# A kernel of linear attention and four experts: the order of a two-bank product, of a first quarter's copies and of two low halves

## The chip, the cores and the metric

One core of one Trainium2 chip runs the whole kernel. The metric is the device time of one execution in microseconds (us); less is better. Several executions of one kernel are taken and their median is quoted.

## The reference, cut to what matters

```python
def _attn_ref(q, k, v, omega):           # q, k, v: 4 x 8 x 576 x 64; omega: 128 x 64
    q_p, k_p = phi(q * scale), phi(k * scale)   # exp(x omega^T - |x|^2/2 - max)
    kv = einsum('bhsm,bhsd->bhmd', k_p, v); z = sum(k_p, axis=2)
    return einsum('bhsm,bhmd->bhsd', q_p, kv) / (einsum('bhsm,bhm->bhs', q_p, z)[..., None] + 1e-06)

def _moe_ref(x, domain_probs, w1, w2):   # x: 2304 x 512, w1: 4 x 512 x 1024, w2: 4 x 1024 x 512
    p = domain_probs / (domain_probs.sum(-1, keepdims=True) + 1e-09)
    for e in range(4):
        h = np.maximum(x @ w1[e], 0.0)
        out += p[:, e:e + 1] * (h @ w2[e])
```

The attention's output, 2304 tokens by 512, is the x of the experts. All data are float32.

## The kernel before, in words

**Matrix products.** Each float32 operand of an expert is split in two, a high part (rounded, type fp32r) and a low part (what is left), and a product is made of three matmuls: high by high, high by low, low by high. A split is one ACT copy (the high half) and one subtraction on POOL or DVE (the low half).

**Stages.** The tokens are handled in three blocks. The first 512 tokens (with the attention of the first batch) and the next 768 come first, while the other batches' attention runs beside them. The last block, 1024 tokens, is done by `deep` (L1084), and the change is in `deep` alone. `deep` runs eight times, once for each expert and half of its hidden features; the text calls these passes 1 to 8. Pass 1 begins at about 560.4 us, each later one some 39.9 us after the one before it.

**One pass.** Both of the expert's products are made by a scheme of seven products in place of eight, on quarters of the operands. In the last block the second product is turned: the weights are the stationary operand and the hidden values, 512 tokens wide, the moving one, so that a result tile has output features on partitions and fills one PSUM bank (128 x 512 float32). All eight banks come from one pool (L46); a bank is free again when the last instruction that reads it is done, and the oldest free one is given out first.

The order of the work is written out by hand (L1180 to L1298), and every engine runs its instructions in that order. A `product(g, p, where)` (L1107) is six matmuls into a bank; with `start=False` it adds to what the bank holds. The first ten products of a pass are, in order: (0,1), (0,2), (0,5), (0,6), (1,1), (1,2), (0,7), (1,5), (0,3), (0,4); the text counts them first to tenth. The fourth, seventh and tenth add to bank `u` of the first product, with (0,6), (0,7), (0,4). The helpers between them are:

- `keep` (L1119): an ACT copy of a bank to a `sum` tile. `keep(0,"u","u2")` (L1189) copies bank `u` after the fourth product; the seventh product writes that bank and so waits for this copy.
- `added` (L1123) adds a kept sum to a bank on DVE, `scaled` (L1128) takes the maximum with 0 and multiplies by the experts' shares on DVE. They give the quarters a11, a12, a21 and so on. a21 (L1208) reads bank `u` after the seventh product and goes to a new bank; the tenth product writes bank `u` and so waits for a21's `added`.
- `high` (L1134): ACT copy of a quarter, to the high half of a hidden tile (`hs`) or to `r11`. `low` (L1137): the subtraction on DVE that makes the low half.
- `prepare` (L1103): one or no step of the weights' preparation (`w2_sides`, L683) for this pass: ACT copies and POOL subtractions (`w2h`, `w2l`, `w2s`, `w2f`). The steps differ in pass 1 (L1098): there the step behind `keep(0,"b5","p5")` is `plain(3)`, an ACT copy with its POOL subtraction, and in the others it is sums on POOL.

The second product is `times(to, a, b)` (L1140): for two halves f of the hidden features and two banks i, three matmuls each, twelve in all. `into` (L1150) adds the two banks to SBUF tiles on DVE, bank 0 first. The groups in order: `xl` begun with a11 and b11 (L1235, L1240, one f at a time), `xr` from T1 (L1260), `z` (L1265, reads a12 and b12 in `hs[2]` and `hs[3]`), `xr` from A22 (L1272), `xl` left (L1282), `xl` right (L1289), and a last one from T1 with one bank at a time (L1295). The last three use the two banks of `xl` one after the other with `into` in between (L1283, L1290, L1296); the text calls the passages from left to right and from right to last the two junctions. `z` takes two new banks: the first is that which a22 had, the second that which b22 had, so its first matmul waits for the last reader of b22, `low(b22, ...)` (L1257).

```python
        def times(to, a, b, fs=(0, 1), start=True, at=(0, 1)):
            for f in fs:
                (xa, xc), (wa, wc) = a[f], b[f]
                for i in at:
                    ps, w = to[i], slice(i * P, (i + 1) * P)
                    for k, (y, x) in enumerate(((wa, xa), (wa, xc), (wc, xa))):
```

Of the kernel before, what the change touches and what calls it, by code (L numbers as in the profile page):

```python
# [14 lines left out]
def attention_moe(ctx, tc, kT, qT, kd, qd, kn, qn, vn, omT, probs, w1, w2, out):  # L15
# [15 lines left out]
    E, FP, P, _ = w1.shape  # L31
# [36 lines left out]
    def bank(name):  # L68
        return psum.tile([P, 512], F32, tag="ps", name=name)

    def f32(ap):
        return ap.bitcast(F32)
# [34 lines left out]
    def held(shape, tag, dtype=F32R, name=None):  # L107
        return moe.tile(shape, dtype, tag=tag, name=name or tag, bufs=BUFS[tag])
# [531 lines left out]
    def split(t, a, c, hi, lo):  # L640
        if hi is nc.scalar:
            hi.activation(a, t, AF.Copy)  # L642
        else:
            hi.tensor_copy(a, t)
        lo.tensor_tensor(c, t, f32(a), ALU.subtract)  # L645
# [438 lines left out]
    def deep(v):  # L1084
# [4 lines left out]
        hs = [tuple(held([P, n], x) for x in ("hh", "hl")) for _ in range(FH)]  # L1089
# [9 lines left out]
        T1, A22 = ((sevens_t[0][:, i], sevens_t[0][:, i + 1]) for i in (0, 2))  # L1099
        t1, t2 = (x.rearrange("p t c -> p (t c)")[:, :2 * n].rearrange("p (k x) -> p k x", k=2) for x in (va, vb))  # L1100
        r11 = att.tile([P, 2, n], F32, tag="q", name="r11", bufs=1)

        def prepare():  # L1103
            for _ in range(steps2.pop(0)):
                next(ready2, None)

        def product(g, p, where, start=True):  # L1107
            if start:
                P_[g][where] = bank("g1")
            ps = P_[g][where]  # L1110
            (wa, wc), (xa, xc) = W[v, "w1", g][p], X[p]
            for k in range(2):
                w = slice(k * P, (k + 1) * P)
                for a, x, at in ((wa, xa, 0), (wa, xc, 1), (wc, xa, 2)):
                    nc.tensor.matmul(  # L1115
                        ps, a[:, w], x[:, k], start=(start and k + at == 0), stop=(k == 1 and at == 2), skip_group_check=not start
                    )

        def keep(g, where, name):  # L1119
            P_[g][name] = t = held([P, 512], "sum", F32)  # L1120
            nc.scalar.activation(t, P_[g][where], AF.Copy)  # L1121

        def added(g, where, name, to=None):  # L1123
            t = P_[g][where] if to is None else to
            nc.vector.tensor_tensor(t, P_[g][where], P_[g][name], ALU.add)
            return t

        def scaled(t, j):  # L1128
            nc.vector.scalar_tensor_tensor(t, t, 0.0, shares[j], ALU.max, ALU.mult)
# [4 lines left out]
        def high(t, to):  # L1134
            nc.scalar.activation(to, t, AF.Copy)  # L1135

        def low(t, hi, to):  # L1137
            nc.vector.tensor_tensor(to, t, f32(hi), ALU.subtract)  # L1138

        def times(to, a, b, fs=(0, 1), start=True, at=(0, 1)):  # L1140
            for f in fs:
                (xa, xc), (wa, wc) = a[f], b[f]
                for i in at:
                    ps, w = to[i], slice(i * P, (i + 1) * P)
                    for k, (y, x) in enumerate(((wa, xa), (wa, xc), (wc, xa))):
                        nc.tensor.matmul(  # L1146
                            ps, y[:, w], x, start=(start and f + k == 0), stop=(f + k == 3), skip_group_check=not start
                        )
# [35 lines left out]
        prepare()  # L1184
        product(0, 5, "b5")
        keep(0, "b5", "p5")
        prepare()
        product(0, 6, "u", start=False)
        keep(0, "u", "u2")  # L1189
# [2 lines left out]
            store(0)  # L1192
        product(1, 1, "u")
        keep(1, "u", "p1")
        a11 = added(0, "b2", "p1")
        scaled(a11, 0)
        high(a11, hs[0][0])
        high(a11, r11[:, 0])
        low(a11, *hs[0])
        prepare()  # L1200
        product(1, 2, "b2")
        a12 = added(1, "b2", "p1")
        scaled(a12, 0)
        high(a12, hs[2][0])
        low(a12, *hs[2])
        prepare()
        product(0, 7, "u", start=False)
        a21 = added(0, "u", "p5", bank("t"))  # L1208
        scaled(a21, 1)
        prepare()  # L1210
        product(1, 5, "b5")
# [21 lines left out]

        xl = [bank("g2") for _ in range(2)]
        times(xl, hs[:2], weights(0, L), fs=(0,))  # L1235
        product(1, 7, "u", start=False)
        a22 = added(1, "u", "p5", bank("t"))
        scaled(a22, 1)
        less(t2[:, 1], a22, t1[:, 1])
        times(xl, hs[:2], weights(0, L), fs=(1,))  # L1240
        high(a22, A22[0][:, 1])
        split(t2[:, 1], *hs[1], nc.scalar, nc.gpsimd)
# [3 lines left out]
        b22 = added(1, "b5", "u2")  # L1246
# [6 lines left out]
        less(t2[:, 0], b22, t1[:, 0])  # L1253
        split(t2[:, 0], *hs[0], nc.scalar, nc.gpsimd)
        nc.gpsimd.tensor_tensor(r11[:, 0], t2[:, 0], r11[:, 0], ALU.subtract)
        low(b12, *hs[3])
        low(b22, A22[0][:, 0], A22[1][:, 0])  # L1257

        xr = [bank("g2") for _ in range(2)]
        times(xr, split_of(T1), mixed(1, R))  # L1260
        into(xr, 1, 1)
        into(xl, 0, 0)
# [267 lines left out]
    def emit():  # L1530
        pairs, g1 = begin()
        later = [Halves(b, hp) for b in range(1, B) for hp in range(NP)]
        windows = {
            0: (first_rest(pairs, opening(later[0], both=True)), 20 / 11),
            3: (joint_ticks(later[:-NP]), 76 / 45.4),
            N0: (chain(opening(later[-NP]), later_ticks(later[-NP:])), 54 / (NV * (BIG[1][1] // P + 1) * 0.8)),
        }
        ticks, n, done, per = iter(()), 0, 0.0, 0
        for v in range(len(visits)):
            if v in windows:  # L1540
                for _ in ticks:
                    pass
                ticks, per = windows[v]
                n, done = 0, 0.0
            for share in first_visit(g1) if v == 0 else deep(v) if v in DEEP else fast(v) if v >= N0 else plain(v):
                done += share
                while n < done * per:
                    next(ticks, None)
                    n += 1
        store(0)  # L1550
# [62 lines left out]
```

## Time and profile before

| | |
|---|---|
| median of 3 runs | 887.83 us (887.57 to 887.88) |
| the profiled execution | 887.46 us, of which the span from the first to the last instruction is 885.7 us |
| busy, share of the span | PE 99%, PEld 85%, DVE 65%, POOL 63%, ACT 54% |
| granted TensorE clock | 9 tenths or more of full speed in all 40 slices, mean 0.999 |
| chain that ended last | PE 89%, DVE 6%, ACT 2%, issue 2%, DMA 1% |

PE is the matmul engine, PEld its weight loads, DVE VectorE, ACT ScalarE, POOL GpSimd. In a timeline row stand the start, the time taken, engine, line, operation, the tile written and the tiles read, shape and count; in brackets the idle time of that engine before the row and what ended it. The listed 0.39 us of a matmul holds its way through the array; the next one starts before it ends.

### The profile page before, as it was taken

What the parts mean: (1) busy time and instruction counts of PE and PEld (TensorE: products, weight loads), DVE (VectorE), ACT (ScalarE), POOL (GpSimd) and SP (SyncE); (2) the same over time, 40 slices, a digit from 0 to 9 for tenths busy, and PEclk for the clock granted to TensorE, in tenths of its full rate; (3) what the DMA queues carried; (4) which work ended last, traced back from release to release, by engine and by line L of the source; (5) the groups of instructions that cost most, each with busy time, mean ns of one, the idle gap of its engine ahead of it and who ended that gap; (6) DMA issues with size and microseconds to landing.
All of it is one profiled execution on the core that took longest, in us unless ns stands there. A gap on an engine that the chain in (4) does not pass through costs nothing.

```text
span 885.7 us, 13361 instructions
## 1 busy us (share of the span) xinstructions
PE 873.5 (99%) x4785; PEld 749.6 (85%) x4785; DVE 578.4 (65%) x953; ACT 478.4 (54%) x1076; POOL 561.4 (63%) x526
## 2 busy tenths in 40 slices
PE   9999999999999999999999999999999999999997
PEld 9988888989888898898988989777787777777785
DVE  6766566766678537657585576975766748475755
ACT  6696676776765465554555536444343435343341
POOL 6859474655555445344353447778979787887954
PEclk9999999999999999999999999999999999999999
DMA  7664544534422864545545258715525351525312
GB/s 183 195 216 158 190 134 155 176 90 134 134 73 75 306 215 161 214 140 211 195 156 214 78 196 263 260 36 178 154 88 165 98 163 58 179 69 170 121 45 96
DMA packets 67411, 136.04 MB, mean 154 GB/s; under 512 B 10384, under 2 KB 22896, under 8 KB 67344
## 3 DMA queue, kind: packets, MB, share of 16 engines
q1 hardware_dynamic: 57328, 105.05, 37.0%
q0 software_dynamic: 9360, 29.82, 10.3%
q8 instruction: 38, 0.62, 0.3%
q10 hardware_dynamic: 656, 0.31, 0.1%
q14 instruction: 29, 0.24, 0.1%
HBM read 101.06 MB, written 34.10 MB: 153 GB/s over the span
## 4 chain that ended last, share of the span: by engine, by line
PE 89%; DVE 6%; ACT 2%; issue 2%; DMA 1%; SPq 0%; DVEq 0%
PE g L1146 17%; PE g L967 13%; PE g L1115 12%; PE g L830 8%; PE g L831 8%; PE g L832 8%; PE g L815 3%; PE g L816 3%; PE g L817 3%; PE kv L406 2%; PE k_ps L351 1%; DVE acc L1160 1%; PE q_ps L351 1%; PE qt_ps L417 1%; DVE xbl L645 1%
## 5 line engine op out<-in xcount | busy, mean ns | idle before, releaser
L645 POOL TENSOR_TENSOR w2l<-w2r,w2h 128x512 fp32r<-128x512 f32 x61 | 79.2, 1306 | 76.7 <-ACT w2h L642 66.4
L645 POOL TENSOR_TENSOR w1sl<-w1r,w1sh 128x512 fp32r<-128x512 f32 (+1 forms) x43 | 75.1, 1747 | 59.8 <-ACT w1sh L642 53.4
L830 PE MATMUL g<-w2h,hh 128*128 128x512 f32 x280 | 111.7, 399 | 0.0
L832 PE MATMUL g<-w2h,hl 128*128 128x512 f32 x280 | 109.6, 392 | 0.0
L831 PE MATMUL g<-w2l,hh 128*128 128x512 f32 x280 | 109.6, 391 | 0.0
L1160 DVE TENSOR_TENSOR acc<-g,acc 128x512 f32<-128x512 f32 x104 | 67.6, 684 | 37.1 <-PE g L1146 37.1
L645 POOL TENSOR_TENSOR w1al<-w1r,w1ah 128x512 fp32r<-128x512 f32 (+1 forms) x45 | 49.6, 1118 | 60.1 <-ACT w1ah L642 49.3
L842 DVE SCALAR_TENSOR_TENSOR acc<-g,pr,acc 128x512 f32<-128x512 f32 x70 | 51.0, 735 | 28.0 <-PE g L832 27.9
L832 PEld LDWEIGHTS g<-w2h,hl 128*128 128x128 f32 x280 | 52.5, 188 | 11.5
L1121 ACT ACTIVATE sum<-g 128x512 f32<-128x512 f32 x48 | 28.6, 595 | 61.5 <-PE g L1115 61.5
L830 PEld LDWEIGHTS g<-w2h,hh 128*128 128x128 f32 x280 | 52.6, 188 | 10.1
L831 PEld LDWEIGHTS g<-w2l,hh 128*128 128x128 f32 x280 | 52.7, 188 | 8.9
L645 POOL TENSOR_TENSOR w2s<-w2f,w2s 128x512 fp32r<-128x512 f32 x30 | 38.3, 1302 | 25.7 <-ACT w2s L642 25.7
L981 ACT ACTIVATE hh<-sum 128x384 fp32r<-128x384 f32 x48 | 25.0, 524 | 50.5 <-DVE sum L979 50.1
L645 POOL TENSOR_TENSOR t_hl<-va,t_hl 128x1024 fp32r<-128x1024 f32 x16 | 38.7, 2422 | 20.6 <-ACT t_hl L642 20.6
L985 DVE SCALAR_TENSOR_TENSOR hl<-sum,hh 128x384 fp32r<-128x384 f32 x48 | 27.5, 575 | 36.9 <-ACT hh L981 36.2
L303 DVE RECIPROCAL dn<-dn 128x256 f32<-128x256 f32 (+1 forms) x24 | 46.5, 1943 | 6.7 <-ACT dn L297 6.2
L1138 DVE TENSOR_TENSOR hl<-g,hh 128x512 fp32r<-128x512 f32 x32 | 22.0, 688 | 44.2 <-ACT r L1135 38.9
L1115 PE MATMUL g<-xbh,w1sh 128*128 128x512 f32 x128 | 49.9, 390 | 0.0
L1115 PE MATMUL g<-xbl,w1sh 128*128 128x512 f32 x128 | 49.9, 389 | 0.0
L1115 PE MATMUL g<-xbh,w1sl 128*128 128x512 f32 x128 | 49.8, 389 | 0.0
L645 POOL TENSOR_TENSOR w2l<-w1r,w2h 128x512 fp32r<-128x512 f32 x32 | 44.1, 1391 | 6.5 <-ACT w2h L642 6.4
(254 smaller groups left out, 2697.4 us busy)
## 6 DMA issues: line engine op xcount, KB each, us to landing
w1r<-in_w SPq DMA_DIRECT2D x54, 512.0 KB, 3.6
w2r<-in_w SPq DMA_DIRECT2D x76, 256.0 KB, 3.1
kept<-w1sh SPq DMA_DIRECT2D x16, 512.0 KB, 5.0
kept<-w1sl SPq DMA_DIRECT2D x16, 512.0 KB, 5.6
w1sh<-kept POOLq DMA_DIRECT2D x16, 512.0 KB, 5.0
w1sl<-kept POOLq DMA_DIRECT2D x16, 512.0 KB, 5.7
kept<-w1ah SPq DMA_DIRECT2D x16, 384.0 KB, 4.9
kept<-w1al SPq DMA_DIRECT2D x16, 384.0 KB, 4.9
```

Of the source, the lines that this page charges most:

```text
L303: nc.vector.reciprocal(dn, dn)
L645: lo.tensor_tensor(c, t, f32(a), ALU.subtract)
L830: nc.tensor.matmul(ps, ha[:, ts_], wa, start=(c == 0), stop=False)
L831: nc.tensor.matmul(ps, ha[:, ts_], wc, start=False, stop=False)
L832: nc.tensor.matmul(ps, hc[:, ts_], wa, start=False, stop=(c == FH - 1))
L842: nc.vector.scalar_tensor_tensor(acc[i], ps, sc, acc[i], ALU.mult, ALU.add)
L967: nc.tensor.matmul(ps, a[:, w], x[:, k], start=(start and k + at == 0), stop=(k == 1 and at == 2), skip_group_check=not start)
L985: nc.vector.scalar_tensor_tensor(x, y, 0.0, f32(z), ALU.max, ALU.subtract)
L1115: nc.tensor.matmul(ps, a[:, w], x[:, k], start=(start and k + at == 0), stop=(k == 1 and at == 2), skip_group_check=not start)
L1121: nc.scalar.activation(t, P_[g][where], AF.Copy)
L1146: nc.tensor.matmul(ps, y[:, w], x, start=(start and f + k == 0), stop=(f + k == 3), skip_group_check=not start)
L1160: nc.vector.tensor_tensor(t, ps[i], t, ALU.add)
```

## The change

It does three things, all in `deep`. `times` runs over the banks outside and over the halves f inside, so that a bank gets its six matmuls and then the other bank its six. The five lines of a11 (`added`, `scaled`, two `high`, `low`) stand behind `keep(0,"b5","p5")` rather than behind `keep(1,"u","p1")`, and so ahead of the `prepare` behind the third product, of `keep(0,"u","u2")` and of `keep(1,"u","p1")`. Two low halves exchange places with a neighbour: `low(a12)` comes behind a21's `added`, and `low(b22)` ahead of `low(b12)`.

```diff
         def times(to, a, b, fs=(0, 1), start=True, at=(0, 1)):
-            for f in fs:
-                (xa, xc), (wa, wc) = a[f], b[f]
-                for i in at:
-                    ps, w = to[i], slice(i * P, (i + 1) * P)
+            for i in at:
+                ps, w = to[i], slice(i * P, (i + 1) * P)
+                for f in fs:
+                    (xa, xc), (wa, wc) = a[f], b[f]
                     for k, (y, x) in enumerate(((wa, xa), (wa, xc), (wc, xa))):
...
         product(0, 5, "b5")
         keep(0, "b5", "p5")
+        a11 = added(0, "b2", "p1")
+        scaled(a11, 0)
+        high(a11, hs[0][0])
+        high(a11, r11[:, 0])
+        low(a11, *hs[0])
         prepare()
         product(0, 6, "u", start=False)
         keep(0, "u", "u2")
...
         product(1, 1, "u")
         keep(1, "u", "p1")
-        a11 = added(0, "b2", "p1")
-        scaled(a11, 0)
-        high(a11, hs[0][0])
-        high(a11, r11[:, 0])
-        low(a11, *hs[0])
         prepare()
         product(1, 2, "b2")
         a12 = added(1, "b2", "p1")
         scaled(a12, 0)
         high(a12, hs[2][0])
-        low(a12, *hs[2])
         prepare()
         product(0, 7, "u", start=False)
         a21 = added(0, "u", "p5", bank("t"))
+        low(a12, *hs[2])
         scaled(a21, 1)
...
         nc.gpsimd.tensor_tensor(r11[:, 0], t2[:, 0], r11[:, 0], ALU.subtract)
+        low(b22, A22[0][:, 0], A22[1][:, 0])
         low(b12, *hs[3])
-        low(b22, A22[0][:, 0], A22[1][:, 0])
```

## Rows read from the trace of the kernel before

**Rows 1.** The page, part 1: busy us, share and instructions of each engine

```profile
PE 873.5 (99%) x4785; PEld 749.6 (85%) x4785; DVE 578.4 (65%) x953; ACT 478.4 (54%) x1076; POOL 561.4 (63%) x526
```

**Rows 2.** The waits of PE: who waited for whom, total us, times, longest us

```profile
PE g L1146 <- DVE acc L1160: 2.9, 16, 0.2
PE g L1115 <- DVE t L1125: 2.7, 8, 1.0
```

**Rows 3.** Timeline of PE, pass 6: ninth product's last matmul, tenth's first two

```profile
772.76 0.39 PE L1115 MATMUL g<-xbh,w1sl 128*128 128x512 f32 x1
773.40 0.50 PE L1115 MATMUL g<-xbh,w1ah 128*128 128x512 f32 x1 [0.26 <-DVE t L1125]
773.74 0.40 PE L1115 MATMUL g<-xbl,w1ah 128*128 128x512 f32 x1
```

**Rows 4.** Timeline of the weight loads, pass 6: the tenth product's first load

```profile
773.40 0.19 PEld L1115 LDWEIGHTS g<-xbh,w1ah 128*128 128x128 f32 x1 [0.68 <-DVE t L1125]
```

**Rows 5.** Timeline of DVE, pass 6: a11 scaled, a11 low, a21 added

```profile
764.47 0.70 DVE L1129 SCALAR_TENSOR_TENSOR g<-g,share 128x512 f32<-128x512 f32 x1
...
769.35 0.69 DVE L1138 TENSOR_TENSOR hl<-g,hh 128x512 fp32r<-128x512 f32 x1 [4.18 <-ACT r L1135]
...
772.66 0.69 DVE L1125 TENSOR_TENSOR t<-g,sum 128x512 f32<-128x512 f32 x1
```

**Rows 6.** Timeline of ACT, pass 6: keep p5, keep u2

```profile
765.02 0.60 ACT L1121 ACTIVATE sum<-g 128x512 f32<-128x512 f32 x1 [1.08 <-PE g L1115]
766.38 0.60 ACT L1121 ACTIVATE sum<-g 128x512 f32<-128x512 f32 x1 [0.76 <-PE g L1115]
```

**Rows 7.** Timeline of PE, pass 1: seventh product's first matmul, ninth's last, tenth's first

```profile
568.52 0.39 PE L1115 MATMUL g<-xbh,w1sh 128*128 128x512 f32 x1
...
572.38 0.39 PE L1115 MATMUL g<-xbh,w1sl 128*128 128x512 f32 x1
573.74 0.50 PE L1115 MATMUL g<-xbh,w1ah 128*128 128x512 f32 x1 [0.97 <-DVE t L1125]
```

**Rows 8.** Timeline of DVE, pass 1: a11 scaled

```profile
567.84 0.70 DVE L1129 SCALAR_TENSOR_TENSOR g<-g,share 128x512 f32<-128x512 f32 x1
```

**Rows 9.** Timeline of ACT, pass 1: copy of the preparation, a11's two copies

```profile
565.20 0.63 ACT L642 ACTIVATE w2h<-w1r 128x512 fp32r<-128x512 f32 x1
...
568.57 0.60 ACT L1135 ACTIVATE hh<-g 128x512 fp32r<-128x512 f32 x1 [0.55 <-DVE g L1129]
569.06 0.59 ACT L1135 ACTIVATE r<-g 128x512 f32<-128x512 f32 x1
```

**Rows 10.** Timeline of PE, pass 6: third and fourth matmul of z

```profile
786.27 0.40 PE L1146 MATMUL g<-hh,w2l 128*128 128x512 f32 x1
786.63 0.50 PE L1146 MATMUL g<-hh,w2h 128*128 128x512 f32 x1
```

**Rows 11.** Timeline of DVE, pass 6: low(b12), low(b22)

```profile
785.30 0.68 DVE L1138 TENSOR_TENSOR hl<-g,hh 128x512 fp32r<-128x512 f32 x1
785.90 0.68 DVE L1138 TENSOR_TENSOR t_hl<-g,t_hl 128x512 fp32r<-128x512 f32 x1
```

**Rows 12.** Timeline of PE, pass 6, first junction: left's 9th, 12th; right's first, second

```profile
793.39 0.62 PE L1146 MATMUL g<-hh,w2s 128*128 128x512 f32 x2
...
794.08 0.40 PE L1146 MATMUL g<-hh,w2s 128*128 128x512 f32 x1
794.66 0.47 PE L1146 MATMUL g<-hh,w2s 128*128 128x512 f32 x1 [0.18 <-DVE acc L1160]
794.96 0.39 PE L1146 MATMUL g<-hl,w2s 128*128 128x512 f32 x1
```

**Rows 13.** Timeline of DVE, same junction: into xl, both banks

```profile
793.82 1.38 DVE L1160 TENSOR_TENSOR acc<-g,acc 128x512 f32<-128x512 f32 x2 [1.27 <-PE g L1146]
```

**Rows 14.** Timeline of the weight loads, same junction: right's first load

```profile
794.63 0.19 PEld L1146 LDWEIGHTS g<-hh,w2s 128*128 128x128 f32 x1 [0.58 <-issue]
```

**Rows 15.** Timeline of POOL, pass 6: low half of T1, read by xr from T1

```profile
780.11 2.42 POOL L645 TENSOR_TENSOR t_hl<-va,t_hl 128x1024 fp32r<-128x1024 f32 x1 [1.78 <-ACT t_hl L642]
```

## The prediction

> **What bounds the kernel now.** I read the page's first part, then the waits of PE, then timelines around each of those waits. The first shows PE busy for 99% of the span and no other engine above 85% [rows 1]: time can be won only where PE stands still or starts late. The list of who waits for whom names two waits of PE in the last block: 16 times for the addition of `into` and 8 times for an `added` [rows 2]. These are two and one a pass. The totals there are small, because the listed 0.39 us of a matmul covers most of each hole. The holes have to be read from starts: undisturbed, 17 matmuls lie between the seventh product's first and the ninth product's last, from 568.52 to 572.38 us [rows 7], which is 0.227 us from start to start. Whatever is longer is loss. Three holes stand in every pass.
>
> Hole A, before the tenth product: 0.64 us to its first matmul and 0.34 to the second [rows 3], so 0.98 - 2 x 0.227 = 0.53 us lost, in passes 2 to 8 alike to 0.01. In pass 1 the first step is 1.36 us [rows 7], and with the same 0.11 behind it 1.24 us are lost.
>
> Hole B, inside `z`, before its second bank: 0.36 us [rows 10] and the same 0.11, so 0.24 us, eight times.
>
> Hole C, at the two junctions: 0.58 and 0.30 [rows 12], so 0.88 - 0.45 = 0.43 us, 16 times.
>
> The sum is 7 x 0.53 + 1.24 + 8 x 0.24 + 16 x 0.43 = 3.7 + 1.2 + 1.9 + 6.9 = 13.7 us. No more than this can be won, and the change aims at all three.
>
> **The change part by part.** It adds and removes no instruction; everything is order.
>
> *The product by banks.* Now the left group's first bank ends with its 9th matmul, at 793.39, and the addition starts 0.43 us later, at 793.82, and takes 0.69 a bank [rows 12, 13]; so DVE waits for one bank and not for the whole group. PE reaches the right group about 0.23 us after 794.08, and the bank is not free. With six and six, count from the start of a group: its first bank's last matmul starts at 5 x 0.227 = 1.13, the addition at 1.56, ends at 2.25, and PE's next load came 0.12 after an addition's end (794.51 to 794.63) [rows 13, 14]: 2.37. The load wants to start with the 12th matmul, at 2.50. Margin 0.13 us; the second bank has the same. DVE is free, as it idles 1.27 us before that addition [rows 13] and is asked for it 0.68 us sooner. So hole C goes: -6.9 us, with 0 and -6.9 as ends. I take the whole, since each duration is from a row of the very place.
>
> With this order `z` and the `xr` groups meet their second half f after three matmuls and not after six. T1's low half for `xr` ends at 782.53 [rows 15], and `xr` begins 14 matmuls before 786.27 [rows 10], at 783.09. Both halves f come in one instruction, so the order costs nothing; were that cover of 0.5 us gone, PE would wait for the excess in every pass.
>
> *The exchanged low halves.* `z`'s second bank waits for `low(b22)`, which ends at 786.58 [rows 11]. In first place it ends 0.60 sooner, and the bank is wanted three matmuls later: hole B goes. In return `low(b12)` ends at 786.58, and `z` wants it at its fifth matmul, whose load would start with the fourth, at 786.27 + 0.23 = 786.50. It starts at 786.63, as the fourth does now; the sixth matmul then starts at 786.97 in place of 786.95. Cost 0.02 us a pass; the ends are 0 and the 0.24 of today. -1.9 + 0.2 = -1.7 us.
>
> *The first quarter sooner, passes 2 to 8.* Today ACT makes a11's copies behind `keep(1,"u","p1")`; DVE stands 4.18 us before `low(a11)` until 769.35 [rows 5], and a12's and a21's steps queue behind it, so that a21 is added only at 772.66 to 773.35 while the tenth product wants it by 772.76 [rows 3, 5]. After: a11 is scaled by 765.17 [rows 5], ACT starts the copies 0.49 after the row at 765.02 [rows 6] and 0.49 apart [rows 9], done at about 766.6; `low(a11)` is done at 767.3. The first thing DVE then waits for is the sixth product. Its last matmul is 18 before the ninth product's last, so it starts at 772.76 - 18 x 0.227 = 768.68, and a12's `added` follows some 0.43 later (as in [rows 12, 13]), at 769.1, where today DVE is at `low(a11)` until 770.04. `scaled` takes it to 770.6. a21's `added`, now ahead of `low(a12)`, no longer waits for a12's copy on ACT: it runs from about 770.5 to 771.2, some 1.5 us before it is wanted. Hole A goes: -7 x 0.53 = -3.7 us. `keep(0,"u","u2")`, behind the two copies, ends at about 767.1 in place of 766.98 [rows 6]; the seventh product wants it at 768.7. That wait is hidden by the fifth and sixth product. `low(a12)` is wanted by `z` alone, 14 us later.
>
> *The first quarter sooner, pass 1.* Here the cover is missing. a11 is scaled only at 568.54 [rows 8], because DVE still works on the block before; the edit doesn't change that. So ACT, in order, stands before the first copy until 568.57, as today [rows 9]; but now `plain(3)`'s copy and `keep(0,"u","u2")` stand behind it, which today are done before it. The copies start at 568.57 and 569.06 [rows 9], `plain(3)`'s copy at 569.55 (0.63 long, as in [rows 9]), the keep at 570.07, done at 570.67. The seventh product wants to start at 568.52 [rows 7]. It starts at 570.72, and 0.11 more go with the uncovered load: 2.3 us lost, in place of 1.24. The ends: 1.8 if the preparation's copy slips behind the keep, 2.8 if it waits for a buffer as long as it takes. The tenth product is then in time, as 12 matmuls, 2.7 us, lie between the seventh's end and its start. POOL and SP are passed over only here: `plain(3)`'s subtraction and the weights' sums and load behind it come some 4 us later, and their first reader, the `xr` group from T1, only some 10 us after that; I cost them at nothing. In the other passes the step behind a11 has no ACT copy.
>
> A rule to weigh against this: the weight load. In the trace the held matmul's own load starts with the wait's end, at 773.40, and no sooner [rows 3, 4], so each hole has 0.08 to 0.11 us of load on top of the wait, and these are in my sums. The Trainium skill, "TensorE: Matmul & The Clock Gate", section "Architectural detail: the array is 16× 32×32, not 1× 128×128", says that PE's queue pulls weight loads ahead of matmuls in flight; by that a wait would cost itself alone, the holes would give back about 32 x 0.1 = 3.2 us less, an estimate, and the result would be near 879.6. The row speaks against that here, and I keep the row's figure.
>
> **Sum.** -6.9 - 1.7 - 3.7 + (2.3 - 1.24) = -11.2 us. The profiled execution took 887.46 us, which gives 876.3. It is 0.4 under the median of the runs, 887.83, which gives 876.6. I take 876.5.
>
> **The rivals.** *Pass 1 gets no new hole.* If ACT isn't held there, or the preparation's copy and the keep go ahead, the whole 13.7 come: 874.1 to 874.3. Against it speaks that ACT waited for DVE at just this instruction [rows 9].
>
> *The junctions' margin is not there.* 0.13 us is thin. If loads or wake-ups are later by that much, each of the 32 passages from bank to bank (two junctions, two banks, eight passes) uncovers its load, 0.11 us: 3.5 us back, 880.0. All 6.9 back would be 883.4.
>
> *Slower: what I expect of pass 1 happens in every pass.* The mechanism is one queue: the copy of bank `u` behind a11's copies on ACT. It decides against the change where a11 is scaled later than some 1.6 us after today's 765.17. Then eight holes of 2.3 us, 18.4, stand against 13.6 won: 892.3. Against it: only in pass 1 is DVE still busy with another block; from pass 2 on it idles before `low(a11)`.
>
> *Nothing happens:* the engines follow another order than the one written, and the time stays at 887.8. Nothing in the rows speaks for it.
>
> **How the numbers follow.** The forecast, 875.5 to 877.7 with its unknowns (pass 1 between 1.8 and 2.8, hole B between 0 and half), gets 0.70; no hole in pass 1 0.11; the junctions' margin gone in part or whole 0.12; slower 0.03; nothing 0.02; the remaining 0.02 is for several small waits at once. The range takes in the first rival and most of the second: 874.0 to 880.1. About 0.2%, 1.8 us, is what a measurement of this kernel can tell from no change; all cases but the last ones lie far below that: faster 0.95, same 0.02, slower 0.03.
>
> **What the profile should show.** PE's list of waits without `into` in it; the starts at both junctions and inside `z` 0.23 to 0.25 us apart; passes 2 to 8 some 38.3 us from one to the next in place of 39.9; the tenth product unhindered. In pass 1 a wait of PE for the ACT copy of L1121, about 2.2 us long, before the seventh product, and ACT's order there: two copies of a11, one `w2h`, the keep. I am wrong if the junctions still show steps of over 0.3 us, if the keep in passes 2 to 8 ends after the sixth product, or if the granted clock, 0.999 before, is lower in the last block.

## The result and the profile after

The changed kernel took 876.44 us (median of 4 runs, 875.65 to 877.37) against 887.70 us for the kernel before beside it: ratio 0.9877, 95% interval 0.986 to 0.9894. The medians differ by 11.3 us, and by the ratio the change is 1.2% faster. Predicted were 876.5 us, in a range from 874.0 to 880.1. The profiled execution took 876.04 us, its span 874.0.

First the waits of PE in the changed kernel (who waited for whom, total us, times, longest us):

```profile
PE g L1115 <- ACT sum L1121: 2.0, 1, 2.0
PE warm L1312 <- DVE om_r L1303: 1.1, 1, 1.1
PE k_ps L158 <- POOL k L151: 0.9, 1, 0.9
PE g L815 <- DVE hl L822: 0.2, 1, 0.2
```

Both waits of [rows 2] are gone. One new one stands there, for the ACT copy of L1121, once, 2.0 us long; the other three lie ahead of the last block. The chain that ended last shows the same (start, us, what; a stretch that holds the whole of pass 7):

```profile
793.52 14.96 PE g L1115 x66
808.48 1.36 PE g L1146 x6
809.84 1.36 PE g L1115 x6
811.20 1.36 PE g L1146 x6
812.56 2.72 PE g L1115 x12
815.28 16.56 PE g L1146 x72
```

There is no DVE, no ACT and no "issue" left in it: in a later pass PE alone sets the time. To compare kernels without what happens ahead of the last block, which varies by up to 1.3 us between the profiled executions (the block's first matmul starts between 560.37 and 561.62), I use the starts of matmuls: from the first of L1115 to the last of L1146, and from one pass's first to the next's. Before, that is 560.37 to 880.31, 319.94 us; after, 561.04 to 869.79, 308.75: 11.19 less. Passes 2 to 7 (six steps) take 39.93 us each before and 38.33 after, and pass 1 takes 40.62 before and 40.63 after.

**The tenth product, pass 6.** PE's timeline after, to be held against [rows 3]:

```profile
767.02 0.39 PE L1115 MATMUL g<-xbh,w1sl 128*128 128x512 f32 x1
767.25 0.39 PE L1115 MATMUL g<-xbh,w1ah 128*128 128x512 f32 x1
767.48 0.39 PE L1115 MATMUL g<-xbl,w1ah 128*128 128x512 f32 x1
```

The steps are 0.23 and 0.23 where they were 0.64 and 0.34. Pass 6 starts 5.74 us earlier in this trace (755.01, before 760.75); that is the shift to keep in mind in the next two. DVE after, against [rows 5]:

```profile
758.73 0.70 DVE L1129 SCALAR_TENSOR_TENSOR g<-g,share 128x512 f32<-128x512 f32 x1
760.90 0.69 DVE L1138 TENSOR_TENSOR hl<-g,hh 128x512 fp32r<-128x512 f32 x1 [1.47 <-ACT r L1135]
763.44 0.70 DVE L1125 TENSOR_TENSOR g<-g,sum 128x512 f32<-128x512 f32 x1 [1.85 <-PE g L1115]
764.17 0.70 DVE L1129 SCALAR_TENSOR_TENSOR g<-g,share 128x512 f32<-128x512 f32 x1
764.78 0.69 DVE L1125 TENSOR_TENSOR t<-g,sum 128x512 f32<-128x512 f32 x1
765.53 0.69 DVE L1138 TENSOR_TENSOR hl<-g,hh 128x512 fp32r<-128x512 f32 x1
```

The scaling of a11 stands at the same place in the pass as before (758.73 + 5.74 = 764.47). Its low half comes 2.7 us sooner, DVE then waits for PE and no more for ACT, and a21 is added until 765.47, 1.55 us before 767.02. The prediction said some 1.5.

**Pass 1.** PE, ACT and DVE after, against [rows 7 to 9]; the pass begins 0.67 us later in this trace:

```profile
568.98 0.39 PE L1115 MATMUL g<-xbh,w1al 128*128 128x512 f32 x1
571.40 0.50 PE L1115 MATMUL g<-xbh,w1sh 128*128 128x512 f32 x1 [2.03 <-ACT sum L1121]
571.74 0.40 PE L1115 MATMUL g<-xbl,w1sh 128*128 128x512 f32 x1
```

```profile
565.38 0.60 ACT L1121 ACTIVATE sum<-g 128x512 f32<-128x512 f32 x1 [1.60 <-PE g L1115]
569.26 0.60 ACT L1135 ACTIVATE hh<-g 128x512 fp32r<-128x512 f32 x1 [3.28 <-DVE g L1129]
569.75 0.59 ACT L1135 ACTIVATE r<-g 128x512 f32<-128x512 f32 x1
570.23 0.63 ACT L642 ACTIVATE w2h<-w1r 128x512 fp32r<-128x512 f32 x1
570.75 1.09 ACT L1121 ACTIVATE sum<-g 128x512 f32<-128x512 f32 x2
```

```profile
568.52 0.70 DVE L1129 SCALAR_TENSOR_TENSOR g<-g,share 128x512 f32<-128x512 f32 x1
```

This is one wait told by three engines. ACT stands 3.28 us before a11's first copy because DVE scales a11 only until 569.22; the preparation's copy and the copy of bank `u` come behind it, the latter done at 571.35; at 571.40 the seventh product starts, 2.42 us after the matmul before it, and the next follows 0.34 later. Lost: 2.42 + 0.34 - 2 x 0.227 = 2.3 us.

**Inside `z` and at a junction, pass 6**, against [rows 10, 12, 13]. First `z`'s fourth to sixth matmul, then DVE at the two junctions:

```profile
780.21 0.39 PE L1146 MATMUL g<-hh,w2h 128*128 128x512 f32 x1
780.44 0.42 PE L1146 MATMUL g<-hl,w2h 128*128 128x512 f32 x1
780.69 0.39 PE L1146 MATMUL g<-hh,w2l 128*128 128x512 f32 x1
```

```profile
783.81 2.47 DVE L1160 TENSOR_TENSOR acc<-g,acc 128x512 f32<-128x512 f32 x4
786.63 0.69 DVE L1160 TENSOR_TENSOR acc<-g,acc 128x512 f32<-128x512 f32 x1 [0.36 <-PE g L1146]
788.03 0.69 DVE L1160 TENSOR_TENSOR acc<-g,acc 128x512 f32<-128x512 f32 x1 [0.70 <-PE g L1146]
789.42 0.69 DVE L1160 TENSOR_TENSOR acc<-g,acc 128x512 f32<-128x512 f32 x1 [0.70 <-PE g L1146]
```

In `z` the longest step left is 0.25, behind the fifth matmul, which reads `low(b12)`: 0.02 us lost, as worked out. At the junctions the additions now come singly, one every 1.39 us, and DVE idles 0.70 between them: it is PE that sets the beat. The cover worth watching is the 0.36 us before the first of them; the four additions ahead of it end that close. PE has some to spare too: the addition of the left group's first bank ends at 787.32, and the load of the right group's first matmul can start with the left's last, at 787.60.

### The profile page after: what moved, and what is told of

Same layout as the page of the kernel before. It is cut to its first block, busy times and chain, and to the rows that moved or that the text cites. A ratio compares the mean times of both kernels' runs of the same rounds, so it can differ in the third digit from the quotient of the medians.

```text
span 874.0 us, 13367 instructions
## 1 busy us (share of the span) xinstructions
PE 865.7 (99%) x4785; PEld 750.7 (86%) x4785; DVE 577.4 (66%) x953; ACT 478.8 (55%) x1076; POOL 561.1 (64%) x526
## 4 chain that ended last, share of the span: by engine, by line
PE 95%; DVE 2%; DMA 1%; issue 1%; ACT 0%; POOL 0%; SPq 0%; POOLq 0%; DVEq 0%
PE g L1146 18%; PE g L1115 17%; PE g L967 13%; PE g L830 8%; PE g L831 8%; PE g L832 8%; PE g L815 3%; PE g L816 3%; PE g L817 3%; PE kv L406 2%; PE k_ps L351 2%; PE q_ps L351 1%; PE qt_ps L417 1%; DVE xbl L645 1%; PE q_ps L158 1%; PE nd L290 1%
## 5 line engine op out<-in xcount | busy, mean ns | idle before, releaser
L832 PEld LDWEIGHTS g<-w2h,hl 128*128 128x128 f32 x280 | 52.6, 188 | 11.5 <-DVE hl L822 0.2
L1121 ACT ACTIVATE sum<-g 128x512 f32<-128x512 f32 x48 | 28.7, 600 | 47.4 <-PE g L1115 46.7
L1115 PE MATMUL g<-xbh,w1sh 128*128 128x512 f32 x128 | 49.9, 390 | 2.0 <-ACT sum L1121 2.0
L1115 PE MATMUL g<-xbl,w1sh 128*128 128x512 f32 x128 | 49.8, 389 | 0.0
L1115 PE MATMUL g<-xbh,w1sl 128*128 128x512 f32 x128 | 49.8, 389 | 0.0
L979 DVE TENSOR_TENSOR sum<-g,sum 128x384 f32<-128x384 f32 x48 | 26.5, 555 | 32.7 <-PE g L967 27.6
```

The costliest lines, as they stand in the source:

```text
L832: nc.tensor.matmul(ps, hc[:, ts_], wa, start=False, stop=(c == FH - 1))
L1115: nc.tensor.matmul(ps, a[:, w], x[:, k], start=(start and k + at == 0), stop=(k == 1 and at == 2), skip_group_check=not start)
```

## The experiments

All times are medians. "Last block" is the length from the trace of the profiled execution, reckoned as above; 319.94 us before, 308.75 for the changed kernel.

| kernel | us | ratio to before, 95% interval | last block, us | less than before |
|---|---|---|---|---|
| banks alone | 878.32 | 0.9895 (0.9881 to 0.9908) | 311.25 | 8.7 |
| `low(b22)` alone | 885.36 | 0.9975 (0.9966 to 0.9984) | 318.09 | 1.9 |
| `low(a12)` alone | 882.54 | 0.9942 (0.9929 to 0.9954) | 314.97 | 5.0 |
| a11 alone | 884.45 | 0.9967 (0.9955 to 0.998) | 317.17 | 2.8 |
| the change again | 877.03 | 0.9879 (0.9866 to 0.9893) | 310.44 | 9.5 |
| the change without a11 | 873.97 | 0.9846 (0.9833 to 0.986) | 306.95 | 13.0 |
| banks and `low(a12)` | 874.52 | 0.9851 (0.9837 to 0.9864) | 306.68 | 13.3 |
| a11 behind the keep | 874.29 | 0.985 (0.9837 to 0.9864) | 307.03 | 12.9 |
| a11 two steps late | 878.78 | 0.9909 (0.9892 to 0.9926) | 311.81 | 8.1 |
| a11 five steps late | 893.94 | 1.0079 (1.0064 to 1.0094) | 326.38 | -6.4 |

**The product by banks alone.** The two loops of `times` are exchanged, and nothing else of the change is made.

> The product by banks alone. Theory (three separate holes): the holes at the junctions go (16 x 0.43 = 6.9 us), and the one inside z goes too (1.9 us), since the second bank is now wanted three matmuls later and its old release is in time; hole A stays: 887.7 - 8.8 = 878.9 us, with starts of 0.23 us at both junctions and 0.64 before the tenth product. Rival (the hole in z needs the exchange of low halves): 887.7 - 6.9 = 880.8 us, with 0.3 us or more inside z.

Measured: 878.32, the last block 8.7 us shorter. PE's waits name no `into` any more, and hole A is left as it was:

```profile
PE g L1115 <- DVE t L1125: 2.8, 8, 1.0
```

`z` runs without a hole in it; here are its fourth to sixth matmul (PE's timeline):

```profile
782.34 0.39 PE L1146 MATMUL g<-hh,w2h 128*128 128x512 f32 x1
782.57 0.39 PE L1146 MATMUL g<-hl,w2h 128*128 128x512 f32 x1
782.79 0.39 PE L1146 MATMUL g<-hh,w2l 128*128 128x512 f32 x1
```

So the order by banks closes holes B and C both, and the theory stands against its rival.

**The exchange of `low(b22)` and `low(b12)` alone.**

```diff
+        low(b22, A22[0][:, 0], A22[1][:, 0])
         low(b12, *hs[3])
-        low(b22, A22[0][:, 0], A22[1][:, 0])
```

> The exchange of low(b22) and low(b12) alone. Theory: z's second bank is free 0.60 us sooner, the hole in z goes, nothing else: 887.7 - 1.9 = 885.8 us, junctions still 0.58 us. Rival (the hole only moves to the matmul that reads low(b12)): 887.7 us, with a step of 0.3 us at z's later matmuls.

Measured: 885.36, the last block 1.85 us shorter. The hole in `z` is gone (third, fourth and fifth matmul start at 786.05, 786.28 and 786.51), the junctions are as before. The rival, that the hole only moves on, falls.

**`low(a12)` behind a21's `added`, alone.** a11 stays where it was.

```diff
         high(a12, hs[2][0])
-        low(a12, *hs[2])
         prepare()
         product(0, 7, "u", start=False)
         a21 = added(0, "u", "p5", bank("t"))
+        low(a12, *hs[2])
```

> low(a12) behind a21's added, alone; a11 stays in its old place. Theory: a21's added no longer waits for a12's copy on ACT and starts as soon as a12 is scaled, ending near 572.0 in pass-6 terms where it is wanted 0.7 us later; hole A goes in passes 2 to 8 (3.7 us) and in pass 1 as well (1.2 us), with no new hole there: 887.7 - 4.9 = 882.8 us. Rival (hole A comes from a11's late low half and goes only with a11's move): 887.7 us, with 0.6 us still before the tenth product.

Measured: 882.54, the last block 4.97 us shorter. In this kernel's DVE timeline, pass 6, a11's low half is as late as ever, and still a21 is in time, since the next step of DVE no longer waits for ACT:

```profile
767.30 0.69 DVE L1138 TENSOR_TENSOR hl<-g,hh 128x512 fp32r<-128x512 f32 x1 [4.18 <-ACT r L1135]
767.91 0.69 DVE L1125 TENSOR_TENSOR g<-g,sum 128x512 f32<-128x512 f32 x1
768.63 0.70 DVE L1129 SCALAR_TENSOR_TENSOR g<-g,share 128x512 f32<-128x512 f32 x1
769.24 0.69 DVE L1125 TENSOR_TENSOR t<-g,sum 128x512 f32<-128x512 f32 x1
```

a21 is added by 769.93, and the ninth product's last matmul starts at 770.71. One moved line closes hole A in all eight passes. Pass 1 still takes 0.26 us more than the later ones (39.63 against 39.37): a step of 0.33 us stands in it before the product (1,7), which comes back in three kernels below.

**The move of a11's five lines alone.** `low(a12)` stays ahead of a21's `added`.

> The move of a11's five lines alone; low(a12) stays ahead of a21's added. Theory: passes 2 to 8 lose hole A (3.7 us), a21 being added some 0.1 to 0.2 us before it is wanted; pass 1 gets a hole of 2.3 us before the seventh product in place of its 1.24 before the tenth: 887.7 - 3.7 + 1.1 = 885.1 us. Rival (both moves are needed): hole A stays in part, 886.5 to 888.8 us.

Measured: 884.45, the last block 2.77 us shorter (predicted 2.6). Hole A goes in this way too, with less to spare (a21 is added from 771.08 to 771.77 in pass 6, with the ninth product's last matmul at 771.97). PE waits once for the ACT copy, 2.0 us, and pass 1 takes 41.71 us, 1.09 more than before. So each of the two moves closes hole A by itself, and a11's has the price of a new hole.

**The changed kernel again**, beside the next three.

> The changed kernel once more, as the measure for the kernels beside it: 876.4 us by both theories, one hole of 2.3 us before the seventh product of pass 1.

Measured: 877.03 (875.91 to 878.05). Its profiled execution, 878.05, is the longest of them; the last section shows what stands in its pass 1.

**The whole change without a11's move.**

Relative to the changed kernel:

```diff
         keep(0, "b5", "p5")
-        a11 = added(0, "b2", "p1")
-        scaled(a11, 0)
-        high(a11, hs[0][0])
-        high(a11, r11[:, 0])
-        low(a11, *hs[0])
         prepare()
...
         keep(1, "u", "p1")
+        a11 = added(0, "b2", "p1")
+        scaled(a11, 0)
+        high(a11, hs[0][0])
+        high(a11, r11[:, 0])
+        low(a11, *hs[0])
         prepare()
```

> The whole change without the move of a11's lines. Theory: low(a12)'s move alone closes hole A in every pass and ACT is not held in pass 1, so all 13.7 us come: 874.0 us, 2.4 under the changed kernel, with no hole of PE over 0.3 us in the last block. Rival (a11's move is what closes hole A in passes 2 to 8): 876.4 + 3.7 - 2.3 = 877.8 us or more, with 0.6 us before the tenth product.

Measured: 873.97 (873.85 to 874.43), 3.1 us under the changed kernel beside it, and none of its runs reaches into that one's. ACT in pass 1 copies bank `u` at 566.63, ahead of a11, and no wait of PE in the last block is left in the list. The last block is 12.99 us shorter, and the holes held 13.7. The rest is in sight: pass 1 takes 38.84 us and the later ones 38.33, because two small holes open in pass 1, one before the product (1,7) and one in the `xl` group right. They show in the weight loads:

```profile
577.35 0.19 PEld L1115 LDWEIGHTS g<-xbh,w1sh 128*128 128x128 f32 x1 [0.36 <-ACT sum L1121]
594.42 0.19 PEld L1146 LDWEIGHTS g<-hl,w2s 128*128 128x128 f32 x1 [0.50 <-POOL hl L645]
```

Their matmuls start 0.32 and 0.46 us after the ones before them, so the expectation of no hole over 0.3 us was missed here. And the later passes are 0.03 us longer than 39.93 less their holes.

**Banks and `low(a12)` alone**, without a11's move and without the exchange.

> Only the product by banks and low(a12)'s move; a11 and the order of low(b22) and low(b12) as before. Theory: the exchange brings nothing on top of the banks, as either closes the hole in z: 874.0 us, the same as without a11's move. Rival (the exchange is needed): 875.9 us, with 0.3 us inside z.

Measured: 874.52; the last block takes 306.68 us, 0.27 less than with the exchange. On top of the order by banks the exchange brings nothing; it costs 0.05 us in a later pass (38.29 against 38.33). Half of that is the 0.25 step in `z`, the rest lies in the steps of `z` behind it, 0.23 us each where they are 0.227 without the exchange; why these are longer is not shown. The two small holes of pass 1 stand here too (steps of 0.33 and 0.50 us).

**a11 one step later**, behind `keep(0,"u","u2")`, in all passes.

Relative to the changed kernel the same five lines are taken out, and put back here:

```diff
         product(0, 6, "u", start=False)
         keep(0, "u", "u2")
+        a11 = added(0, "b2", "p1")
+        scaled(a11, 0)
+        high(a11, hs[0][0])
+        high(a11, r11[:, 0])
+        low(a11, *hs[0])
         prepare()
```

> The changed kernel with a11's five lines one step later, behind the copy of bank u (keep u2), in all passes. Theory: the copy is ahead of a11's copies on ACT and is not held, so the hole in pass 1 goes and nothing else changes: 874.1 us. Rival (the hole in pass 1 comes from something else on DVE or POOL at the block's beginning): 876.4 us, with the 2.3 us still there.

Measured: 874.29 (874.10 to 874.98). ACT in pass 1 of this kernel:

```profile
566.23 0.60 ACT L1121 ACTIVATE sum<-g 128x512 f32<-128x512 f32 x1 [0.24 <-PE g L1115]
568.74 0.60 ACT L1135 ACTIVATE hh<-g 128x512 fp32r<-128x512 f32 x1 [1.92 <-DVE g L1129]
569.24 0.59 ACT L1135 ACTIVATE r<-g 128x512 f32<-128x512 f32 x1
569.71 0.61 ACT L1121 ACTIVATE sum<-g 128x512 f32<-128x512 f32 x1
```

ACT waits for DVE just as long as it must, but the copy that PE needs is ahead of that wait. The hole is gone, and ACT's order is what differs from the changed kernel: the preparation's copy and the copy of bank `u` now stand ahead of a11's. So the hole came from this queue. The two small holes of pass 1 stand here as well (0.33 and 0.47 us), so the last block is 1.7 us shorter than in the changed kernel (307.03 against 308.75) and not 2.3.

**a11 scaled later.** Steps without effect on the values stand between `added` and `scaled`, two in one kernel and five in another.

```diff
         a11 = added(0, "b2", "p1")
+        for _ in range(2):
+            nc.vector.tensor_scalar(a11, a11, 0.0, None, ALU.max)
         scaled(a11, 0)
```

> The changed kernel with two idle DVE steps (maximum with 0, some 0.73 us each) between a11's added and scaled, so that a11 is scaled 1.46 us later. Theory (the copy of bank u waits behind a11's copies on ACT; passes 2 to 8 have some 1.6 us to spare): no new hole in passes 2 to 8, or one of at most 0.1 us, the hole of pass 1 grows by 1.46: 876.4 + 1.5 = 877.9 us, up to 878.6. Rival (passes 2 to 8 have no such wait behind a11): also 877.9.

> The same with five idle DVE steps, 3.65 us. Theory: passes 2 to 8 now get the hole that pass 1 has, 3.65 - 1.6 + 0.11 = 2.1 us each before the seventh product, 14.9 us, and pass 1 grows by 3.65: 876.4 + 14.9 + 3.7 = 895 us, more than the kernel before. Rival (no such queue in passes 2 to 8): 876.4 + 3.7 = 880.1 us.

Measured with two: 878.78. In the later passes there is no new hole (38.33 us each), in pass 1 the wait is 3.5 us long in place of 2.0, as expected by both theories. The time is 0.2 us over the bound of 878.6; the last section shows a fall of the granted clock in this kernel that costs more than that. Measured with five: 893.94 against 895 expected, slower than before (1.0079, 1.0064 to 1.0094), so the rival's 880.1 falls. PE's waits in it:

```profile
PE g L1115 <- ACT sum L1121: 16.1, 8, 5.7
```

and the seventh product of pass 6, where the hole is 1.88 + 0.34 - 0.45 = 1.77 us, against 2.1 expected:

```profile
775.28 0.39 PE L1115 MATMUL g<-xbh,w1al 128*128 128x512 f32 x1
777.16 0.50 PE L1115 MATMUL g<-xbh,w1sh 128*128 128x512 f32 x1 [1.49 <-ACT sum L1121]
777.50 0.39 PE L1115 MATMUL g<-xbl,w1sh 128*128 128x512 f32 x1
```

So a11 had some 2.0 us to spare in the later passes (3.67 us of added steps less a wait of 1.66), not 1.6: the 1.6 is counted from the copies, and these start 0.35 us after a11 is scaled anyway (759.43 and 759.78 in the changed kernel's pass 6), behind `keep(0,"b5","p5")`. Beyond that point the change loses in each of the eight passes what it lost in one. This is the prediction's rival on the slower side, brought about by added steps: its mechanism exists, and its condition doesn't hold in the kernel as changed.

## Why the prediction was right

The forecast was 876.5, the result 876.44, and the terms came out one by one. In the last block of the profiled executions, predicted against measured: the order by banks and the exchange 6.9 + 1.7 = 8.6 (8.7 measured for the order by banks alone, without the 0.02 step); a11's move 2.6 (2.8 alone); together 11.2 (11.19). The two measured alone add up to 11.5; the 0.3 us between are what the exchange costs on top of the order by banks.

*Luck.* That forecast and median agree to 0.06 us is luck in part. The four runs go from 875.65 to 877.37, and the median of the second four is 877.03. A lower granted clock in the last block was named as a sign of being wrong: it didn't show in the first profiled execution and did in the second (last section), and no term of the sum stands for it. What the prediction earned is the 11.2 us of the sum against 11.19 measured from the profiled executions before and after, both at full granted clock in the last block's matmuls.

*Holes read from starts.* The list of waits gave 2.9 and 2.7 us, the starts 13.7. The kernel without a11's move got 13.0 of them back, and pass 1's two small holes account for most of the rest. The list counts only what the listed end of a matmul leaves uncovered.

*The weight load.* I kept 0.08 to 0.11 us of load in each hole. The Trainium skill ("TensorE: Matmul & The Clock Gate", section "Architectural detail: the array is 16× 32×32, not 1× 128×128") says that PE's queue pulls weight loads ahead of matmuls in flight. Where PE runs undisturbed, the trace agrees: in pass 1 after, the load for the matmul of 568.75 starts at 568.53, one matmul ahead. Behind a wait it doesn't: the load of the held matmul starts at 571.40, with that matmul, and the next one follows 0.34 us later, as behind hole A before [rows 3, 4].

```profile
571.40 0.19 PEld L1115 LDWEIGHTS g<-xbh,w1sh 128*128 128x128 f32 x1 [2.46 <-ACT sum L1121]
```

One step of the prediction is wrong here, without touching the forecast: that by the other rule the holes would give back 3.2 us less. The 13.7 us were read from starts, so whatever a load costs in a hole is in them by either rule; only the 0.11 us behind the new hole hang on it. The total can't tell the two apart, the row does.

*Pass 1.* The new hole was predicted at 2.3 us between the seventh product's 568.52 and 570.72, and measured at 2.3, with ACT in the order foretold: two copies of a11, one `w2h`, the keep. In the profiled execution pass 1 came out even, 40.63 against 40.62, because hole A (1.24) went as well and so did the holes in `z` and at the junctions (0.24 + 2 x 0.43).

*Margins.* a21 had 1.55 us (said: 1.5). a11 had some 2.0 ahead of the copy of bank `u` (said: 1.6); the error was on the safe side. At the junction of pass 6, 0.28 us lie between the addition's end and the time at which PE can load (787.32 and 787.60); less the 0.12 that the prediction counts for the way from one to the other, that is 0.16 (said: 0.13). The rival that this margin fails didn't come true.

*What the prediction did not see* is that the change does the same thing twice. Either the order by banks or the exchange closes the hole in `z`, and either a11's move or `low(a12)`'s closes hole A. It credited hole A to both moves together; `low(a12)`'s was enough, and beside it a11's move only brought the new hole. The rival "pass 1 gets no new hole", 874.1 to 874.3, is what three kernels of this study reach: 873.97, 874.52 and 874.29. Their runs overlap, so none is shown to be the fastest, but all three are below every run of the changed kernel.

## What to carry to other kernels

Read the stalls of a saturated matmul engine from the starts of its instructions, pass by pass, and not from the totals of its waits. When a step is moved up in a hand-written order, look at what now stands behind it on each in-order queue, first of all in the pass that follows another stage, where its input may be late; here one step further down closed the hole and left only two small ones. And when several edits aim at one stall, try each alone: two of the three holes here were closed twice over, and both doubles had a price, 2.3 us once for a11's move and 0.05 us a pass for the exchange.

## What was not expected of the hardware

The hole of 2.3 us in pass 1 can cost more than its length. In the second set of runs of the changed kernel the profiled execution (878.05 us) shows a granted clock below full speed behind it, and its matmuls there start 0.43 us apart. The stretches (us, PE, PEld, DVE, ACT, POOL busy with counts, granted clock, DMA share, GB/s) and PE's timeline:

```profile
568.00:573.00 5.00, 2.98 (x13) 2.10 (x12) 2.98 (x6) 2.58 (x5) 1.81 (x2) 0.98 0.90 340
573.00:577.00 4.00, 4.00 (x12) 3.17 (x11) 2.44 (x4) 2.46 (x4) 3.79 (x6) 0.60 0.33 95
577.00:580.00 3.00, 3.00 (x14) 2.44 (x13) 2.27 (x4) 0.19 (x1) 1.09 (x1) 1.00 0.48 169
```

```profile
572.68 0.54 PE L1115 MATMUL g<-xbl,w1sh 128*128 128x512 f32 x1
573.02 0.63 PE L1115 MATMUL g<-xbh,w1sl 128*128 128x512 f32 x1
573.44 0.63 PE L1115 MATMUL g<-xbh,w1sh 128*128 128x512 f32 x1
```

0.427 us for 512 columns is the lower of the two levels, 1.2 GHz. No matmul had started from 569.24 to 571.65; the first longer step begins at 572.68, and the last ends at 576.34. The nine steps between are 1.6 us longer than nine of 0.227, and the last block took 310.44 us there against 308.75: 1.7 us more for the same hole.

Five of the profiled executions have a hole of 2.4 us or more (from start to start) in pass 1. Three of them show the fall: this one, the kernel with two late steps (0.58 between 573 and 577 us; its eight longer steps cost 1.6 us, more than the 0.2 us over its bound) and the one with five (0.70 there, and 0.83 from 577 to 580). The other two, the first execution of the changed kernel (876.04 us) and the kernel with a11's move alone, have a hole of 2.42 us and a granted clock of 1.00 behind it. Where the hole was taken away, in the kernels without a11's move, with banks and `low(a12)` alone and with a11 behind the keep, the profiles show 1.00 there. What decides whether the clock falls behind a hole of 2.4 us is not shown.

In the eight runs of the two sets, the three of 875.65 to 876.04 us have a mean granted clock of 1.0, the two of 876.39 and 876.84 one of 0.999, and the three of 877.37 to 878.05 one of 0.997 or 0.998. So the fall may be what spreads them, but only two of the eight were profiled, and a mean of 0.999 alone says little: the profiled execution without a11's move has it too, with the granted clock at 1.00 up to 868 us and at 0.89 from 868 to 872, behind its last matmul.
